# Turning the result by a VectorE block transpose and storing 64 short lines, in place of a PE product, a copy and 16 longer lines

## The chip, the cores and the metric

The kernel runs on one core of one Trainium2 chip. The metric is the device time of one execution in microseconds (us), median of several. Since the change concerns the last 2.5 us of 420, I also use a second measure, read from each trace: **the tail**, from the start of the VectorE instruction that reads the last product (tile `mT`) to the last semaphore count of the store.

Names: PE is the matrix engine, PSUM the memory that its products go to, SBUF the on-chip memory with 128 partitions; DVE is VectorE, ACT ScalarE, POOL GpSimd. SP is the engine that issues the loads and stores; an "issue" is its instruction for one of them. A "line" is one contiguous run of bytes of a transfer, and a "packet" is what the trace records of a DMA engine's work: here one line, or one count of the semaphore.

## The reference, cut to what matters

The program is one decode step for two sequences: a conditioning vector makes six modulation vectors, attention runs over a cache of 32768 keys and values, then an MLP. Only its last line matters here:

```python
x = x + ga * _A_ref(h, A_k_cache, A_v_cache, A_wq, A_wo)
h = _layernorm(x, axis=-1) * (1 + cb) + sb
x = x + gb * _B_ref(h, B_w1, B_b1, B_w2, B_b2)
return x            # bfloat16, (2, 1, 1024)
```

The result is 2 x 1024 bfloat16 numbers, 4 KB.

## The kernel before

The MLP's second product ends in PSUM with the features on partitions: feature 128k + p of sequence b stands at partition p, column (k, b). Memory wants a sequence's features one behind the other, so the result is turned, by a PE product with the identity, before it is stored.

```python
    for g in range(16, FT):                  # last product, waits for the last load
        ...
            pe(... e.matmul(psO[:, 2 * k:2 * k + 2], lhsT=w[:, j, k * 128:(k + 1) * 128], rhs=gT[:, g, 0:2], ...)
    dve(lambda e: e.tensor_tensor(mT[:, :, :], psO[:, 0:16].rearrange("p (k b) -> p k b", b=2), mod(5), ALU.mult), ...)
    dve(lambda e: e.tensor_tensor(res_bf.rearrange("p b k -> p k b"), mT[:, :, :], x1b[:, :, :], ALU.add), ...)
    pe(lambda e: e.matmul(psM[0:16, 0:128], lhsT=res_bf.rearrange("p b k -> p (b k)"), rhs=ident[:, :], start=True, stop=True), ...)
    dve(lambda e: e.tensor_copy(res16[:, :], psM[0:16, 0:128]), ...)

    s_out = nc.alloc_semaphore("s_out")
    T.wait("sp", reads=["res16"])
    T.raw("sp", lambda e: e.dma_start(out.rearrange("b o (k p) -> (b o k) p", p=128), res16[:, :]).then_inc(s_out, 16))
    ...
    nc.sync.wait_ge(s_out, 16)               # the program ends when the store has landed
```

`x1b` is the residual with the bias, ready some 13 us earlier.

## Time and profile before

| | before |
|---|---|
| time, three runs | 420.12 us (420.05 to 420.15) |
| span of the profiled run | 418.7 us |
| read from memory | 178.28 MB, 426 GB/s |
| last load's product, on PE | 413.27 to 416.18 us |
| two VectorE steps, PE turn, cast | 416.22 to 417.31 us |
| issue of the store to its landing | 1.35 us |

Read it from the bottom up: the kernel is a stream of loads, and after the last one there is a chain in which every instruction waits for the one ahead of it. The lines are shown in the prediction.

### The profile page before, as it was taken

What the parts mean: (1) busy time and instruction counts of PE and PEld (TensorE: products, weight loads), DVE (VectorE), ACT (ScalarE), POOL (GpSimd) and SP (SyncE); (2) the same over time, 40 slices, a digit from 0 to 9 for tenths busy, and PEclk for the clock granted to TensorE, in tenths of its full rate; (3) what the DMA queues carried; (4) which work ended last, traced back from release to release, by engine and by line L of the source; (5) the groups of instructions that cost most, each with busy time, mean ns of one, the idle gap of its engine ahead of it and who ended that gap; (6) DMA issues with size and microseconds to landing.
All of it is one profiled execution on the core that took longest, in us unless ns stands there. A gap on an engine that the chain in (4) does not pass through costs nothing.

```text
span 418.7 us, 11609 instructions
## 1 busy us (share of the span) xinstructions
PE 291.0 (70%) x5183; PEld 231.3 (55%) x5183; DVE 209.6 (50%) x423; ACT 149.4 (36%) x179; POOL 6.8 (2%) x29
## 2 busy tenths in 40 slices
PE   1407449766996895699369957976995699564536
PEld 1104219762993794299149926962894399221214
DVE  1201105546677676467726664766477567620411
ACT  2000015533565364256405632643365166400100
POOL 3000000000000000000000000000000000000000
PEclk9999557986896997799589958986697889576585
DMA  9989999999999999999999999999999999899995
GB/s 373 450 380 449 448 404 493 398 406 446 441 432 429 423 451 429 419 454 457 391 435 476 407 416 448 438 438 426 438 438 426 416 460 457 377 448 428 424 427 249
DMA packets 5581, 178.42 MB, mean 426 GB/s; under 512 B 698, under 2 KB 706, under 8 KB 964
## 3 DMA queue, kind: packets, MB, share of 16 engines
q1 hardware_dynamic: 5572, 178.28, 98.8%
q8 instruction: 8, 0.13, 0.1%
q14 instruction: 1, 0.01, 0.0%
HBM read 178.28 MB, written 0.00 MB: 426 GB/s over the span
## 4 chain that ended last, share of the span: by engine, by line
DMA 71%; PE 24%; DVE 2%; issue 1%; ACT 1%; SPq 1%
DMA V<-in_A_v_cache_dram 39%; DMA wo<-in_A_wo_dram 10%; DMA K<-in_A_k_cache_dram 10%; PE psZ L584 10%; DMA w<-in_B_w_dram 9%; PE psKT L536 8%; DMA wmod<-in_w_mod_dram 4%; PE psS L548 1%; PE psZ L548 1%; PE psS L655 1%; PE psZ L729 1%; PE psZ L469 1%; ACT KT_sb L540 0%; PE psS L469 0%; DVE m1c L553 0%
## 5 line engine op out<-in xcount | busy, mean ns | idle before, releaser
L536 PE MATMUL psKT<-ident,K 128*128 128x128 bf16 x2048 | 163.1, 229 | 11.5 <-DMA K<-in_A_k_cache_dram 11.5
L540 ACT ACTIVATE KT_sb<-psKT 128x1024 bf16<-128x1024 bf16 x96 | 98.2, 1025 | 124.4 <-PE psKT L536 124.4
L542 DVE COPY KT_sb<-psKT 128x1024 bf16<-128x1024 bf16 x160 | 106.7, 688 | 61.6 <-PE psKT L536 61.2
L536 PEld LDWEIGHTS psKT<-ident,K 128*128 128x128 bf16 x2048 | 126.7, 102 | 13.0 <-DMA K<-in_A_k_cache_dram 12.7
L584 PE MATMUL psZ<-V,E_sb 128*32 128x512 bf16 x512 | 46.4, 541 | 23.2 <-DMA V<-in_A_v_cache_dram 20.0
L548 PE MATMUL psS<-qcur,KT_sb 128*128 128x8 bf16 x1024 | 44.7, 167 | 2.2 <-issue 2.2
L584 PEld LDWEIGHTS psZ<-V,E_sb 128*32 128x32 bf16 x512 | 18.7, 130 | 47.7 <-issue 38.8
L548 PE MATMUL psZ<-qcur,KT_sb 128*128 128x8 bf16 x1024 | 43.0, 167 | 2.2 <-issue 1.5
L548 PEld LDWEIGHTS psS<-qcur,KT_sb 128*128 128x128 bf16 x1024 | 40.0, 97 | 2.3 <-issue 2.3
L548 PEld LDWEIGHTS psZ<-qcur,KT_sb 128*128 128x128 bf16 x1024 | 37.9, 96 | 3.4 <-issue 1.6
L572 ACT ACTIVATE E_sb<-S_sb 128x512 bf16<-128x512 f32 x32 | 19.5, 630 | 29.6 <-DVE S_sb L570 29.6
L570 DVE TENSOR_TENSOR S_sb<-S_sb,gmb 128x512 f32<-128x512 f32 x32 | 20.0, 685 | 0.3
L576 DVE TENSOR_REDUCE rs<-E_sb 128x8 f32<-128x512 bf16 x32 | 19.7, 675 | 0.0
L469 PE MATMUL psS<-wmod,inT 128*32 128x512 bf16 x32 | 5.1, 624 | 16.2 <-DMA wmod<-in_w_mod_dram 16.2
L553 DVE TENSOR_REDUCE m1c<-psZ 128x8 f32<-128x512 f32 x16 | 11.1, 693 | 10.2 <-ACT S_sb L552 10.1
L595 DVE RECIPROCAL rinv<-psM 128x1 f32<-128x1 f32 x8 | 1.3, 168 | 27.7 <-PE psM L593 27.7
L605 PE MATMUL psM<-msum,hmat 128*128 128x128 f32 x16 | 4.2, 347 | 13.3 <-DVE msum L600 13.3
L559 PE MATMUL psM<-identf,m 128*8 128x128 f32 x16 | 4.3, 369 | 13.1 <-DVE m L556 13.1
L553 DVE TENSOR_REDUCE m1c<-psS 128x8 f32<-128x512 f32 x16 | 11.1, 693 | 3.2 <-ACT S_sb L552 3.1
L552 ACT ACTIVATE S_sb<-psZ 128x512 f32<-128x512 f32 x16 | 9.5, 595 | 7.5 <-PE psZ L548 7.5
L477 DVE COPY S_sb<-psS 128x512 f32<-128x512 f32 x1 | 0.7, 690 | 22.9 <-PE psS L469 22.9
L469 PEld LDWEIGHTS psS<-wmod,inT 128*32 128x32 bf16 x32 | 1.1, 132 | 19.3 <-DMA wmod<-in_w_mod_dram 18.0
(123 smaller groups left out, 167.5 us busy)
## 6 DMA issues: line engine op xcount, KB each, us to landing
K<-in_A_k_cache_dram SPq DMA_DIRECT2D x16, 4096.0 KB, 27.1
wq<-in_A_wq_dram SPq DMA_DIRECT2D x2, 4096.0 KB, 44.8
wo<-in_A_wo_dram SPq DMA_DIRECT2D x2, 4096.0 KB, 39.0
w<-in_B_w_dram SPq DMA_DIRECT2D x2, 3584.0 KB, 32.5
wmod<-in_w_mod_dram SPq DMA_DIRECT2D x1, 6144.0 KB, 29.8
w<-in_B_w_dram SPq DMA_DIRECT2D x3, 2048.0 KB, 37.8
wmod<-in_w_mod_dram SPq DMA_DIRECT2D x1, 4608.0 KB, 15.8
wmod<-in_w_mod_dram SPq DMA_DIRECT2D x1, 1536.0 KB, 6.0
```

The costliest lines, as they stand in the source:

```text
L469: pe(lambda e, w=it.view, k=k, kk=kk, ch=ch, n=n, q=q: e.matmul(bank[n][32 * q:32 * q + 32, :], lhsT=inT[:, k, :], rhs=w[:, kk, ch * 512:( ...
L536: pe(lambda e, kq=kq, jj=jj, w=kt, t=t: e.transpose(psKT[kq][:, jj * 128:(jj + 1) * 128], w[:, t, :], ident[:, :]), reads=[it.reg, "ident" ...
L540: act(lambda e, src=src: e.activation(KT_sb[g8][:, :, :], src, ACT.Copy), reads=[f"psKT{kq}"], writes=[f"KT_sb{g8}"], sem=f"ev{cc}_{g8}")
L542: dve(lambda e, src=src: e.tensor_copy(KT_sb[g8][:, :, :], src), reads=[f"psKT{kq}"], writes=[f"KT_sb{g8}"], sem=f"ev{cc}_{g8}")
L548: pe(lambda e, t=t, jj=jj: e.matmul(ps[:, t * HPG:(t + 1) * HPG], lhsT=KT_sb[g8][:, jj, :], rhs=qcur[:, :], start=True, stop=True), reads= ...
L552: act(lambda e: e.activation(Sc, ps.rearrange("p (t h) -> p h t", h=HPG), ACT.Copy), reads=[preg], writes=[f"S_sb_{cc}"], sem=f"sc{cc}")
L553: dve(lambda e: e.tensor_reduce(m1c[:, :, cc], ps.rearrange("p (t h) -> p h t", h=HPG), AX.X, ALU.max), reads=[preg], writes=[f"m1c{cc}"])
L559: pe(lambda e: e.matmul(psM[0:HPG, 0:128], lhsT=m1[:, :], rhs=identf[:, :], start=True, stop=True), reads=["m1", "identf"], writes=["psM"])
L570: dve(lambda e: e.tensor_tensor(Sc, Sc, gmb[:, :].unsqueeze(2).to_broadcast([128, HPG, TPC]), ALU.subtract), reads=[f"S_sb_{cc}", "gmb"], ...
L572: act(lambda e: e.activation(Ec, Sc.rearrange("p h (u t) -> p u h t", t=4), ACT.Exp, scale=SCALE), reads=[f"S_sb_{cc}"], writes=[f"E_sb_{c ...
L576: dve(lambda e: e.tensor_reduce(rs4[:, :, cc], Ec.rearrange("p u h t -> p h u t"), AX.XY, ALU.add), reads=[f"E_sb_{cc}"], writes=[f"rs4_{c ...
L584: pe(lambda e, t4=t4, tg=tg, q=q: e.matmul(psO[32 * q:32 * q + 32, :], lhsT=E_sb[:, tg // 4, :, :].rearrange("p h t -> p (h t)"), rhs=vt[: ...
```

## The change

The intent is to take the detour over PE and PSUM out of that chain. One VectorE instruction transposes 32x32 blocks within the partitions, so four blocks of 32 partitions are turned at once; the 16 columns are spread to 32, every second one zero, so that one even step selects the 64 lines. Each line has 32 numbers, 64 bytes, and the store puts them at their places.

```diff
-    res_bf = sb("res_bf", [128, 2, KT8], BF16)
-    res16 = c16
+    res_bf = sb("res_bf", [128, 2, KT8, 2], BF16)
+    resT = sb("resT", [128, 32], BF16)
@@ (at the start)
+    T.inst("pool", lambda e: e.memset(res_bf[:, :, :, :], 0.0), writes=["res_bf"])
@@ (at the end; the semaphore wait is on resT then)
-    dve(... tensor_tensor(res_bf.rearrange("p b k -> p k b"), mT, x1b, ALU.add) ...)
-    pe(... matmul(psM[0:16, 0:128], lhsT=res_bf.rearrange("p b k -> p (b k)"), rhs=ident[:, :], ...) ...)
-    dve(... tensor_copy(res16[:, :], psM[0:16, 0:128]) ...)
+    dve(... tensor_tensor(res_bf[:, :, :, 0].rearrange("p b k -> p k b"), mT, x1b, ALU.add) ...)
+    dve(... transpose(resT[:, :], res_bf.rearrange("p b k e -> p (b k e)")) ...)
-    T.raw("sp", ... dma_start(out.rearrange("b o (k p) -> (b o k) p", p=128), res16[:, :]) ...)
+    T.raw("sp", ... dma_start(out.rearrange("b o (k q r) -> q (b o k) r", q=4, r=32), resT[0:128:2, :]) ...)
```

More of the change, by code (lines that the diff above doesn't have):

```diff
@@ L732, in bass_adaLN_cond__gqa_block_cached__mixer_channel_mlp__decode_kernel @@
     dve(lambda e: e.tensor_tensor(mT[:, :, :], psO[:, 0:16].rearrange("p (k b) -> p k b", b=2), mod(5), ALU.mult), reads=["psO", "modT"], writes=["mT"])
-    dve(lambda e: e.tensor_tensor(res_bf.rearrange("p b k -> p k b"), mT[:, :, :], x1b[:, :, :], ALU.add), reads=["mT", "x1b"], writes=["res_bf"])
-    pe(lambda e: e.matmul(psM[0:16, 0:128], lhsT=res_bf.rearrange("p b k -> p (b k)"), rhs=ident[:, :], start=True, stop=True),
-       reads=["res_bf", "ident"], writes=["psM"])
-    dve(lambda e: e.tensor_copy(res16[:, :], psM[0:16, 0:128]), reads=["psM"], writes=["res16", "c16"])
+    dve(lambda e: e.tensor_tensor(res_bf[:, :, :, 0].rearrange("p b k -> p k b"), mT[:, :, :], x1b[:, :, :], ALU.add), reads=["mT", "x1b"], writes=["res_bf"])
+    dve(lambda e: e.transpose(resT[:, :], res_bf.rearrange("p b k e -> p (b k e)")), reads=["res_bf"], writes=["resT"])
     s_out = nc.alloc_semaphore("s_out")
-    T.wait("sp", reads=["res16"])
-    T.raw("sp", lambda e: e.dma_start(out.rearrange("b o (k p) -> (b o k) p", p=128), res16[:, :]).then_inc(s_out, 16))
+    T.wait("sp", reads=["resT"])
+    T.raw("sp", lambda e: e.dma_start(out.rearrange("b o (k q r) -> q (b o k) r", q=4, r=32), resT[0:128:2, :]).then_inc(s_out, 16))
     with nc.Block(no_gpsimd_drain=True) as block:
```

## The prediction

> **What bounds the kernel now.** I read the page first, then the chain of waits in its last stretch, then the timeline of the last 2.5 us, then the DMA view of the last 1.4 us. The page's summary of the chain that ended last says what the whole kernel is made of, and its DMA rows say how the store behaves:
>
> ```profile
> span 418.7 us, 11609 instructions
> ...
> DMA 71%; PE 24%; DVE 2%; issue 1%; ACT 1%; SPq 1%
> ```
>
> The kernel reads 178.28 MB at 426 GB/s and is a stream of loads with some PE work that isn't hidden. Nothing of the change touches that stream. So the question is what happens after the last load has landed. The timeline of the end shows it (start, duration, then engine, line and tile):
>
> ```profile
> 413.27 2.91 PE L729 MATMUL psZ<-gT,w 128*128 128x2 bf16 x96 [0.30 <-DMA w<-in_B_w_dram]
> 416.22 0.17 DVE L732 TENSOR_TENSOR mT<-psZ,modT 128x16 f32<-128x16 f32 x1 [5.17 <-PE psZ L729]
> 416.43 0.23 DVE L733 TENSOR_TENSOR res_bf<-mT,x1b 128x16 bf16<-128x16 f32 x1
> 416.72 0.09 PEld L734 LDWEIGHTS psM<-ident,res_bf 128*16 128x16 bf16 x1 [0.62 <-DVE res_bf L733]
> 416.72 0.28 PE L734 MATMUL psM<-ident,res_bf 128*16 128x128 bf16 x1 [0.53 <-DVE res_bf L733]
> 417.03 0.28 DVE L736 CAST c<-psM 16x128 bf16<-16x128 f32 x1 [0.37 <-PE psM L734]
> 417.34 0.35 SPq L740 DMA_DIRECT2D out_dram<-c  x1
> ```
>
> Here the reader is to see that every instruction waits for the one above it: nothing overlaps from 416.22 us on. The chain of waits in the same stretch lists the same five steps with the small gaps between the engines, which is why I count the gaps too:
>
> ```profile
> 416.43 0.24 DVE res_bf L733
> 416.68 0.04 issue
> 416.72 0.29 PE psM L734
> 417.01 0.02 issue
> 417.03 0.28 DVE c L736
> ```
>
> After that comes the store, and it is a third of this tail. It is issued at 417.34 us and its row of DMA issues gives 1.4 us to landing, which ends at 418.7 us, the end of the span. The waits of the queue's own engine end on it too:
>
> ```profile
> out_dram<-c SPq DMA_DIRECT2D x1, 4.0 KB, 1.4
> ...
> SPq L744 <- DMA out_dram<-c: 0.6, 1, 0.6
> ```
>
> The second line is the last wait of the program: SP waits for the store's semaphore. All engines have met at the end of the block 0.6 us earlier, so freeing PE or VectorE earlier there gains nothing by itself; only an earlier landing does. The DMA view of 417.3 to 418.7 us, 40 slices of 35 ns, shows where the 1.4 us go:
>
> ```profile
> DMA  0000000000000000000000000111100000000000
> GB/s 0 0 0 0 0 0 0 0 0 0 0 0 0 0 0 0 0 0 0 0 0 0 0 0 0 37 15 37 22 8 0 0 0 0 0 0 0 0 0 0
> DMA packets 32, 0.00 MB, mean 3 GB/s; under 512 B 32, under 2 KB 32, under 8 KB 32
> ```
>
> Some 0.85 us pass before the first packet, 32 packets (16 of 256 bytes and 16 small ones that count the semaphore) lie within five slices, some 0.17 us, and another 0.35 us pass until the last count has arrived. In the packet records a 256-byte packet took 15 ns and a counting one 9 ns, so the 0.17 us are mostly the start of one engine after the other.
>
> **What the Trainium skill says.** (1) "VectorE: DVE Perf Modes", section "The three transpose paths": a VectorE transpose of 128x128 bf16 takes 311 ns against 390 ns by TensorE, it transposes 32x32 blocks only and writes to SBUF. The trace before has one such transpose, in f32 out of PSUM (L704, 128x896, 1.12 us), which agrees in kind: 896 elements at about 1.04 ns are 0.93 us, which leaves some 0.19 us of fixed cost. (2) "DMA: Bandwidth & Descriptors", section "Why a DMA increments its semaphore by 16 and not by 1": a DMA is spread over the largest k up to 16 engines that divides the slowest dimension of both access patterns. The trace agrees for the store of before: 16 lines on either side, 16 data packets and 16 counts. [...](4) The same page, "Specifications": below 512 bytes a transfer is a read-modify-write. No record here shows it; the lines of before, 256 bytes, are already below, so the change doesn't cross that limit.
>
> **The change part by part.** *Removed:* the gap of 0.04 us to PE, the product (0.29 us in the chain), the gap of 0.02 us back and the cast (0.28 us): 0.63 us, from 416.68 to 417.31 us. The semaphore hop to SP (417.31 to 417.34 us) stays.
>
> *Added on the path:* one VectorE transpose, 128x32 bf16. From L704 I take 0.19 us fixed plus 32 x 1.04 ns = 0.03 us, so 0.22 us. The skill's 311 ns for 128 columns, less 96 x 1.04 ns, gives 0.21 us. The gap between two dependent VectorE instructions is 0.03 us (L732 ends at 416.40, L733 starts at 416.43). So 0.25 us stand where 0.63 us stood: **0.38 us less**.
>
> *Altered on the path:* L733 writes every second element now. It took 231 ns, while L421 with the same sizes and a bf16 output of adjacent pairs took 175 ns. The old output has stepped single 2-byte writes; the new one has too, but no two share 4 bytes. I count 0 and allow up to 0.06 us less.
>
> *The store:* the result in memory is addressed as 4 x 16 x 32 elements, whose slowest dimension is 4; the SBUF side has 64 lines. By the skill's rule k falls from 16 to 4, so each of four engines gets 16 packets of 64 bytes and one count, in a row. A 64-byte packet is between 9 ns (4 bytes) and 15 ns (256 bytes), say 10 to 12 ns: 17 x 11 = 0.19 us per engine, plus about 0.04 us until the fourth has started (0.145 us for 16 engines before, 0.01 us each), so 0.23 us where 0.17 us stood: 0.06 us more. Had k stayed 16, it would be about 0.2 us, hardly different. To this I add another 0.07 us, a guess, for writing out four times as many descriptors and for the receipts of 16 writes per engine instead of one. In all the store costs **about 0.13 us more**, with room for 0.4.
>
> *Hidden:* a POOL memset of 128x32 bf16 at the start. The inT memset of 128x256 took 0.31 us and ended at 2.45 us, and its first reader on VectorE runs at 7.98 us, held by a load; 0.1 us more on POOL isn't seen. SBUF addresses behind the buffer move by some tens of bytes; I count 0.
>
> *Sum:* -0.38 + 0.13 = -0.25 us. The time before is 420.12 us (three runs within 0.10 us), so **419.87 us**.
>
> **The rivals.** *First: the store gives it all back.* 64 short lines on four engines take 0.4 us longer than 16 lines on sixteen, by slower descriptor making or by slow partial writes to memory. For it: the time to landing is most of the tail, and its 0.85 us before the first packet are a stage of which the trace shows nothing inside. Against it: loads of 128 lines were issued in 0.33 us, hardly different from the 0.35 us of this 16-line store, and packets are small against the fixed parts. It would make 420.1 to 420.5 us. *Second: the store costs nothing more*, since the short packets overlap with the receipts and the start of sixteen engines falls away; with the faster L733 the gain is 0.4 to 0.45 us, so 419.7 us. *Third: another wait takes the place of the removed one*: the meeting of the engines at the end of the block. It ends 0.6 us before the landing now, and starts earlier with the store, so it can't become the last. *Fourth: the stream moves by itself*, through shifted buffers or the TensorE clock (0.50 granted in the last stretch, 0.81 in the mean). A shift of one part in a thousand is 0.4 us, more than the whole effect; three runs of before within 0.1 us speak against it within one kernel, but not between two builds.
>
> **Range and chances.** The removed part is known to 0.05 us, the store's addition lies between 0 and 0.4 us, and the stream can add about 0.3 us either way. That gives 419.4 to 420.4 us for 8 in 10. Two per cent are 8.4 us, while the whole tail after the last product is 2.5 us, so faster by over 2% is out of reach by this change, and slower by as much needs an accident outside it: 0.99 for the same.
>
> **What would show it.** Right: after L733 a VectorE transpose of 0.20 to 0.24 us, 0.03 us behind it; no PE instruction after L729; the store's issue 0.35 to 0.45 us sooner after the end of L729; 68 packets in the last 1.5 us if k is 4 (80 if it is 16), within 0.2 to 0.3 us; 1.5 us to landing. Wrong: a time to landing of 1.8 us or more (first rival), or a start of L732 that differs from 416.22 us by more than 0.3 us (fourth).

## The result, and the profile after

The changed kernel takes 420.21 us (420.15 to 420.38, six runs), the kernel before in the same rounds 420.13 us (420.04 to 420.23). The ratio is 1.0003, with a 95% interval of 0.9990 to 1.0016: the same, and the 0.08 us between the medians is not clear of the noise.

The timeline of the end, changed kernel (start, duration, engine, line, operation and tile):

```profile
416.19 0.17 DVE L733 TENSOR_TENSOR mT<-psZ,modT 128x16 f32<-128x16 f32 x1 [5.18 <-PE psZ L730]
416.40 0.23 DVE L734 TENSOR_TENSOR res_bf<-mT,x1b 128x16 bf16<-128x16 f32 x1
416.66 0.21 DVE L735 STREAM_TRANSPOSE resT<-res_bf 128x32 bf16<-128x32 bf16 x1
416.90 0.65 SPq L739 DMA_DIRECT2D out_dram<-resT  x1
```

PE is gone from the chain and the transpose is as short as hoped: the store is issued at 416.90 instead of 417.34 us. Counted from the start of `mT`, that is 0.711 us instead of 1.115, so **0.404 us are gained**. But the issuing instruction itself is busy for 0.65 us instead of 0.35. The DMA view of 416.9 to 418.3 us, which starts with the issue and has 40 slices of 35 ns like the one of before:

```profile
DMA  0000000000000000000000000000000000000233
GB/s 0 0 0 0 0 0 0 0 0 0 0 0 0 0 0 0 0 0 0 0 0 0 0 0 0 0 0 0 0 0 0 0 0 0 0 0 9 26 35 33
```

The first packets lie in slice 36, some 1.28 us after the issue, where the kernel before had 0.85 us. The wider view counts 68 packets, 64 of data and 4 that count the semaphore: four engines share the store. The last packet starts 0.171 us after the first (0.157 before), and the last count arrives 0.394 us after that (0.347 before). Together the landing comes 1.843 us after the issue instead of 1.352: **0.491 us are given back**, of which 0.430 lie ahead of the first packet. The tail is 2.554 us instead of 2.467.

### The profile page after: what moved, and what is told of

Read it like the earlier page. It is cut to its first block, busy times and chain, and to the rows that moved or that the text cites. A ratio compares the mean times of both kernels' runs of the same rounds, so it can differ in the third digit from the quotient of the medians.

```text
span 418.8 us, 11608 instructions
## 1 busy us (share of the span) xinstructions
PE 288.9 (69%) x5182; PEld 231.1 (55%) x5182; DVE 209.6 (50%) x423; ACT 149.1 (36%) x179; POOL 6.8 (2%) x30
## 4 chain that ended last, share of the span: by engine, by line
DMA 79%; PE 18%; issue 1%; DVE 1%; SPq 1%; ACT 1%
DMA V<-in_A_v_cache_dram 47%; DMA K<-in_A_k_cache_dram 10%; DMA wo<-in_A_wo_dram 10%; PE psZ L585 9%; DMA w<-in_B_w_dram 9%; PE psKT L537 4%; DMA wmod<-in_w_mod_dram 4%; PE psS L549 1%; PE psZ L730 1%; PE psZ L549 1%; PE psZ L470 1%; PE psS L656 0%; PE psS L470 0%; SPq L648 0%; ACT KT_sb L541 0%
## 5 line engine op out<-in xcount | busy, mean ns | idle before, releaser
L537 PE MATMUL psKT<-ident,K 128*128 128x128 bf16 x2048 | 161.3, 227 | 13.0 <-DMA K<-in_A_k_cache_dram 13.0
L537 PEld LDWEIGHTS psKT<-ident,K 128*128 128x128 bf16 x2048 | 125.0, 101 | 14.4 <-DMA K<-in_A_k_cache_dram 14.4
L585 PE MATMUL psZ<-V,E_sb 128*32 128x512 bf16 x512 | 45.2, 530 | 25.9 <-DMA V<-in_A_v_cache_dram 24.2
```

Of the source, the lines that this page charges most:

```text
L537: pe(lambda e, kq=kq, jj=jj, w=kt, t=t: e.transpose(psKT[kq][:, jj * 128:(jj + 1) * 128], w[:, t, :], ident[:, :]), reads=[it.reg, "ident" ...
L585: pe(lambda e, t4=t4, tg=tg, q=q: e.matmul(psO[32 * q:32 * q + 32, :], lhsT=E_sb[:, tg // 4, :, :].rearrange("p h t -> p (h t)"), rhs=vt[: ...
```

## The experiments

All traces with one store at the end, side by side (e8 has four and is told below). "Plain" is one step from line to line in memory, "nested" are two. Times in us, from the trace's instruction, packet and semaphore records; "first", "last" and "landing" are the first packet, the start of the last packet and the last semaphore count, counted from the start of the issue. "Engines" is the number of counting packets.

| run | lines x bytes | partitions | pattern in memory | engines | issue took | first | last | landing | tail |
|---|---|---|---|---|---|---|---|---|---|
| before | 16 x 256 | neighbours | plain | 16 | 0.346 | 0.848 | 1.005 | 1.352 | 2.467 |
| after | 64 x 64 | every second | nested 4 x 16 | 4 | 0.649 | 1.278 | 1.449 | 1.843 | 2.554 |
| e1 | 64 x 64 | every second | plain | 16 | 0.549 | 1.192 | 1.367 | 1.719 | 2.435 |
| e2 | 62 x 64 | every second | plain | 2 | 0.702 | 1.328 | 1.566 | 2.026 | 2.741 |
| e3 | 64 x 64 | every second | nested 16 x 4 | 16 | 0.644 | 1.289 | 1.459 | 1.815 | 2.528 |
| e4 | 16 x 256 | neighbours | nested 4 x 4 | 4 | 0.740 | 1.374 | 1.491 | 1.832 | 2.894 |
| e5 | 64 x 64 | neighbours | plain | 16 | 0.530 | 1.176 | 1.346 | 1.697 | 2.411 |
| e6 | 16 x 64 | every second | plain | 16 | 0.590 | 1.232 | 1.381 | 1.718 | 2.432 |
| e7, second use | 64 x 64 | every second | nested 4 x 16 | 4 | 0.537 | 1.169 | 1.340 | 1.731 | 2.507 |
| e9 | 16 x 256 | neighbours | plain | 16 | 0.346 | 0.842 | 0.998 | 1.346 | 2.061 |
| e10 | 16 x 128 | neighbours | plain | 16 | 0.346 | 0.838 | 0.994 | 1.325 | 2.039 |
| e11 | 16 x 64 | neighbours | plain | 16 | 0.347 | 0.844 | 0.995 | 1.319 | 2.031 |
| e12 | 16 x 256 | neighbours | plain | 16 | 0.327 | 0.830 | 0.985 | 1.339 | 2.187 |

The table also shows two classes. From the end of the issuing instruction to the first packet ("first" less "issue took") it is 0.49 to 0.50 us in the five rows of 16 plain lines from neighbouring partitions, and 0.63 to 0.65 us in all others. So of the extra time ahead of the first packet, some 0.14 us come after the issue and are alike in every slow form; the rest is in the issue itself and differs from form to form.

The first theories were A, the nested pattern makes the issue long; B, the number of lines; C, the few engines.

**e1: a plain pattern in memory.**

```diff
-  out.rearrange("b o (k q r) -> q (b o k) r", q=4, r=32), resT[0:128:2, :]
+  out.rearrange("b o (n r) -> (b o n) r", r=32), resT[0:128:2, :]
```

> The changed kernel with its 64 lines of 64 bytes laid one behind the other in memory (a wrong order of the result, on purpose): same lines, same SBUF side, but one plain step between lines instead of two nested ones. Theory A (the nested 4 x 16 pattern makes the issue long): issue back at about 0.35 us, first packet 0.85 us after it, landing about 1.4 us after it, and since the issue stays 0.44 us sooner than before, the time is about 0.4 us under the kernel before, 419.75 us. Theory B (64 lines instead of 16): stays at 0.65 us of issue, 1.28 us to the first packet, 1.84 us to the landing, 420.2 us. Theory C (four engines instead of sixteen): as A, since 64 lines on both sides allow 16 engines.

The issue took 0.549 us, the first packet came at 1.192. Between the theories: with a plain pattern and 16 engines the store is only 0.10 us of issue shorter, and far from 0.346. Neither A nor C alone explains the loss. B had said that nothing would change, so it misses 0.10 us too. The time was 420.13 us against 420.06 (ratio 1.0002, interval 0.9988 to 1.0015); the 0.03 us by which the tail is under that of before can't be seen in it.

**e2: 62 plain lines, which only two engines can share.**

```diff
+  out.rearrange("b o (n r) -> (b o n) r", r=32)[0:62, :], resT[0:124:2, :]
```

> As the flat store, but 62 lines, which only 2 engines can share (the last 64 numbers stay unwritten, on purpose). Theory A (nested pattern): issue 0.35 us, first packet 0.85 us after it; the packets then take 31 x 7 ns = 0.22 us per engine. Theory C (few engines): issue 0.65 us or more, first packet 1.28 us or later. Theory B (lines): as C.

0.702 us of issue and 1.328 to the first packet: 0.15 and 0.14 us over e1, whose only other difference is two lines more. So the few engines cost something here, as far as one trace of each shows. The landing is 0.31 us later than in e1: 0.14 us ahead of the first packet, 0.06 us from the first to the last packet (31 lines for each engine), and 0.11 us behind it.

**e3: nested, but shared by 16 engines.**

```diff
+  out.rearrange("b o (n r) -> (b o n) r", r=32).rearrange("(j i) r -> i j r", j=4), resT[0:128:2, :]
```

> 64 lines of 64 bytes in a nested pattern whose slow dimension is 16 (16 x 4 instead of 4 x 16; wrong order on purpose), so that 16 engines share it. Theory A (nested pattern): issue 0.65 us, first packet about 1.28 us after it, 80 packets. Theory C (four engines): issue 0.35 us, first packet 0.85 us after it. Theory B (lines): as A.

0.644 and 1.289 us with 80 packets: like the changed kernel, within 0.01 us, though 16 engines work. So in the nested pattern, four engines in place of sixteen cost nothing ahead of the first packet and 0.03 us at the landing. C is not what costs here; the nesting is worth 0.10 us over e1.

**e4: the kernel before, only its 16 lines permuted, so that the store is nested 4 x 4 (a right result).**

```diff
-  res_bf.rearrange("p b k -> p k b") ...
+  res_bf.rearrange("p b k -> p (b k)").rearrange("p (j b i) -> p i j b", b=2, i=2) ...      # inputs likewise
-  out.rearrange("b o (k p) -> (b o k) p", p=128), res16[:, :]
+  out.rearrange("b o (i j p) -> j (b o i) p", j=4, p=128), res16[:, :]
```

> The kernel before with its PE product and cast, 16 lines of 256 bytes, but the lines permuted so that the store has a nested pattern of 4 x 4 lines (a right result): only the store's pattern changes. Theory A (nested pattern): issue 0.65 us instead of 0.35, first packet 0.4 us later, time 0.4 us over the kernel before, 420.55 us. Theory B (64 lines): nothing changes, 420.13 us. Theory C (four engines): slower as in A, or by the part that the engines make.

The last line of its timeline:

```profile
417.40 0.74 SPq L740 DMA_DIRECT2D out_dram<-c  x1
```

With PE and cast untouched and 16 lines of 256 bytes, the issue takes 0.74 us in place of the 0.35 of before. The landing is 0.48 us later, and the time 420.76 us (420.71 to 420.89) against 420.06, ratio 1.0018 (1.0004 to 1.0031). This run shows in the time itself that the form of a 4 KB store costs something, without VectorE's transpose and without short lines; how much is read from the trace: the landing's 0.48 us, less 0.05 us for a shorter VectorE sum, make the tail 0.43 us longer. The rest of the 0.70 us isn't in the tail. The run doesn't part A from C: with the pattern, the engines fell from 16 to four as well (20 packets), and 16 lines nested over 16 engines were not tried.

B had now failed in e4 and A in e1, so no single one of the two would do, and the step between partitions came in as theory D, the first use of a form as theory W.

**e5: 64 lines from neighbouring partitions.**

```diff
+  out.rearrange("b o (n r) -> (b o n) r", r=32), resT[0:64, :]
```

> As the flat store of 64 lines of 64 bytes, but read from 64 neighbouring partitions instead of every second one (wrong numbers, on purpose). The flat store of e1 took 0.55 us of issue and 1.19 us to the first packet with 64 lines and stepped partitions. Theory B (number of lines): stays at 0.55 and 1.19 us. Theory D (every second partition): falls to about 0.35 and 0.85 us. Theory W (a form of transfer that the program hasn't used before is slow the first time): as D, since plain neighbouring lines are what all loads use.

```profile
417.04 0.53 SPq L739 DMA_DIRECT2D out_dram<-resT  x1
```

0.530 and 1.176 us, only 0.02 less than e1. With 64 lines the step between partitions makes hardly a difference.

**e6: 16 lines from every second partition.**

```diff
+  out.rearrange("b o (n r) -> (b o n) r", r=32)[0:16, :], resT[0:32:2, :]
```

> 16 lines of 64 bytes from every second one of 32 partitions, plain in memory (the rest of the result stays unwritten, on purpose). Theory B (number of lines): 0.35 us of issue, 0.85 us to the first packet. Theory D (every second partition): 0.55 and 1.19 us.

```profile
416.96 0.59 SPq L739 DMA_DIRECT2D out_dram<-resT  x1
```

0.590 and 1.232 us. 16 lines alone don't help either, and this form is a little slower than 64 lines. B can't be the whole cause. Taken with e5, each looks like a refutation of the other theory; what was missing was the run with neither step nor 64 lines (e11).

**e7: the same store once before.**

```diff
+    T.raw("sp", ... dma_start(out.rearrange("b o (k q r) -> q (b o k) r", q=4, r=32), resW[0:128:2, :]).then_inc(s_warm, 16))
+    T.raw("sp", lambda e: e.wait_ge(s_warm, 16))
     T.wait("sp", reads=["resT"])
```

> The changed kernel, and some 40 us before the end, while SP is idle, the same store once from a zeroed buffer, with its own semaphore and waited for (a right result). Theory W (first use is slow): the last store is issued in about 0.4 us, its first packet comes about 0.9 us after, landing about 1.45 us after, the time is 419.8 us. Theories A, B and D (the form itself is slow each time): 0.65, 1.28 and 1.84 us as without it, 420.2 us.

```profile
L742 SPq DMA_DIRECT2D out_dram<-resW x1: 650/650/650, 375.6 to 375.6; - x1
L745 SPq DMA_DIRECT2D out_dram<-resT x1: 537/537/537, 417.2 to 417.2; - x1
```

The first use took 0.650 us, the last 0.537, and its landing came 1.731 us after the issue instead of 1.843. So W has a share of 0.11 us in this run, and most of the extra stays. The store was also issued 0.07 us later after `mT` than in the changed kernel, which the experiment may have brought in itself. The time, 420.21 us against 420.05 (1.0004, 0.9990 to 1.0017), shows no gain.

**e8: four plain stores, two from SP and two from ACT (a right result).**

```diff
+    for q in range(4):
+        T.raw("sp" if q < 2 else "act", lambda e, q=q: e.dma_start(dst4[q], resT[32 * q:32 * q + 32:2, :]).then_inc(s_out if q < 2 else s_out2, 16))
```

> The changed kernel with the store cut into four of 16 lines, one for each block of 32 partitions, two from SP and two from ACT (a right result). If a plain 16-line store costs 0.35 us of issue and 1.35 us to landing (B), the second of each queue lands about 1.7 us after the first issue, 0.14 us sooner than the one nested store: 0.1 us under both kernels in the tail. If stepped partitions are slow (D), the second is issued 0.55 us later and lands about 2.2 us after: 0.35 us slower than the changed kernel.

The tile view of the store (durations in ns, smallest, median and largest):

```profile
L743 SPq DMA_DIRECT2D out_dram<-resT x2: 576/583/590, 417.0 to 417.6; - x2
L743 ACTq DMA_DIRECT2D out_dram<-resT x2: 594/722/849, 417.0 to 417.6; - x2
```

Each issue costs 0.58 us or more again, the second of a queue as well, so first use isn't what makes this form slow here. ACT's second took 0.85 us and landed last: the tail is 3.340 us, the time 421.20 us against 420.05, ratio 1.0028 (1.0015 to 1.0042). A worse version, as D had it, and worse than D's number.

**e9, e10, e11: 16 neighbouring partitions, lines of 256, 128 and 64 bytes, behind the VectorE transpose.**

```diff
-    resT = sb("resT", [128, 32], BF16)
+    resT = sb("resT", [128, 128], BF16)      # e10: 64 columns, e11: 32; zeroed at the start where wider
+    ... out.rearrange("b o (k p) -> (b o k) p", p=128), resT[0:16, :]
+    ... out.rearrange("b o (k p) -> (b o k) p", p=64)[0:16, :], resT[0:16, :]      # e10
+    ... out.rearrange("b o (k p) -> (b o k) p", p=32)[0:16, :], resT[0:16, :]      # e11
```

> The changed kernel with its transpose, but what is stored is 16 lines of 256 bytes from 16 neighbouring partitions of a widened buffer (wrong numbers, on purpose): VectorE's part of the change alone, with the store of the kernel before. So far every store of 64-byte lines took 0.53 to 0.70 us of issue, also with 16 lines, also from neighbouring partitions, also on 16 engines. Theory S (the 64-byte line makes it long): issue 0.35 us, first packet 0.85 us, landing 1.35 us after the issue, which stays 0.4 us sooner than before: the tail from the start of the last product's reader to the landing is 2.06 us, the time 419.7 us. Theory P (what the store reads or when it is issued makes it long, not its form): 0.55, 1.19 and 1.7 us as the other stores after a transpose.

> As the run with 256-byte lines, but 16 lines of 128 bytes (half of the result stays unwritten, on purpose). Theory S with a gradual size effect: between 0.35 and 0.59 us of issue; with a limit between 64 and 128 bytes: 0.35 us; with a limit between 128 and 256: 0.59 us. Theory P: 0.55 us or more.

> As the run with 256-byte lines, but 16 lines of 64 bytes, from 16 neighbouring partitions. Theory S: as the run with stepped partitions, 0.59 us of issue, 1.23 us to the first packet. If the step and not the size made that one slow: 0.35 and 0.85 us. Theory P: 0.55 us or more.

The issue of e9, then that of e11 with its DMA view of 416.92 to 418.32 us, again from the issue on:

```profile
416.98 0.35 SPq L740 DMA_DIRECT2D out_dram<-resT  x1
```

```profile
416.92 0.35 SPq L739 DMA_DIRECT2D out_dram<-resT  x1
...
DMA  0000000000000000000000001010000000000000
GB/s 0 0 0 0 0 0 0 0 0 0 0 0 0 0 0 0 0 0 0 0 0 0 0 0 14 6 6 6 0 0 0 0 0 0 0 0 0 0 0 0
```

All three are issued in 0.35 us, with the first packet in slice 24, after 0.84 us. The length of a line, theory S, does nothing, and where the data come from, theory P, does nothing. **e11 and e6 differ in one thing, 16 partitions side by side against every second of 32**, and that is 0.35 against 0.59 us of issue and 0.401 us in the tail. e11 and e5 differ in 16 against 64 lines: 0.35 against 0.53 us. So the step alone and the number alone each cost some 0.2 us of issue, and both together no more than that (e1: 0.55).

e9 also shows VectorE's part of the change in the time: 419.65 us (419.48 to 419.72) against 420.06, ratio 0.9990 (0.9976 to 1.0003). That interval just reaches 1, but every run of it was under every run of before (419.96 to 420.19), and the 0.41 us of the medians are the 0.406 us of the tails.

**e12: a version meant to beat both, and the forms once more.** No form of the change's store that I found is plain on 16 neighbouring partitions and right, so this goes the other way: keep the store of before and take another step out of the chain. The residual is put into PSUM early by a PE product, and the last product adds to it.

```diff
+    pe(... matmul(psM[0:16, 0:128], lhsT=x1b.rearrange("p b k -> p (b k)"), rhs=identf[:, :], start=True, stop=False, ...))   # early
-    dve(... tensor_tensor(mT, psO, mod(5), ALU.mult)); dve(... tensor_tensor(res_bf, mT, x1b, ALU.add))
+    dve(... tensor_tensor(res_bf[:, :, :], psO[:, 0:16].rearrange("p (k b) -> p b k", b=2), mod(5).rearrange("p k b -> p b k"), ALU.mult))
-    pe(... matmul(psM[0:16, 0:128], lhsT=res_bf..., rhs=ident[:, :], start=True, stop=True))
+    pe(... matmul(psM[0:16, 0:128], lhsT=res_bf..., rhs=ident[:, :], start=False, stop=True, ...))
@@ and 14 stores of 64-byte lines to a scratch tensor, issued by SP behind the last loads
```

> Two things in one kernel. First, a version that should beat both (a right result): the kernel before with its PE product and its store of 16 lines of 256 bytes, but the residual x1b is put into the same PSUM bank by a PE product some 13 us before the end, so that the last product adds to it and the separate VectorE sum (0.23 us and a 0.03 us gap) leaves the path. Expected: 2.20 us from the start of the last product's reader to the landing, against 2.47 before and 2.55 with the change; time 419.85 us. Second, while SP is idle behind the last loads, 14 small stores to a scratch tensor, seven forms with 64-byte lines, each twice, which nothing waits for before the last store: 16 lines from neighbouring partitions, 16 from every second, 32, 64 and 128 from neighbouring ones, the nested 4 x 16 of the change, and a nested 4 x 4 of 16 lines. Only their issue times count, since they queue behind loads. Theory D (a step between partitions is what is slow): 0.35 us for all neighbouring plain ones, more for the second form. Theory L (a line count that was not used before, or 64 itself): 64 lines slow, 16 and 128 fast. Theory W (first use of a form): in each form the second issue is at 0.35 to 0.45 us, whatever the first was. If the form itself costs, first and second agree within 0.1 us, nested forms at 0.55 us or more both times.

Its timeline at the end:

```profile
416.22 0.17 DVE L736 TENSOR_TENSOR res_bf<-psZ,modT 128x16 bf16<-128x16 f32 x1 [5.23 <-PE psZ L733]
...
416.45 0.28 PE L737 MATMUL psM<-ident,res_bf 128*16 128x128 bf16 x1 [0.27 <-DVE res_bf L736]
416.76 0.28 DVE L739 CAST c<-psM 16x128 bf16<-16x128 f32 x1 [0.37 <-PE psM L737]
417.06 0.33 SPq L758 DMA_DIRECT2D out_dram<-c  x1
```

One VectorE instruction less, the store as before: the tail, counted from `res_bf` here, which now reads the last product, is 2.187 us against 2.467. The time is 419.77 us (419.63 to 419.85) against 419.99 (419.87 to 420.09), with a right result. All five runs are under all nine of before, yet the interval of the ratio, 0.9995 (0.9981 to 1.0008), doesn't exclude 1; the tail is the stronger evidence. The scratch stores are in this kernel too, so the version without them was not timed.

The second half of this run failed as a measurement. The tile view of the 14 scratch stores says why:

```profile
L755 SPq DMA_DIRECT2D scratch<-resW x14: 431/990/9895, 377.0 to 411.8; - x14
```

From the fourth on, an issue took up to 9.9 us: SP was held up behind the loads, so the durations are no longer those of the forms. Only the first three, issued at the pace of the loads around them (0.43 us each), may be read, and with care: 16 neighbouring lines 0.431 us (0.347 in e11), 16 with a step 0.594 (0.590 in e6), 32 neighbouring 0.649. The first is as long as the loads just ahead of it, which is 0.08 us over e11. The third hints that 32 lines are slow as well, but stands right before the hold-up.

## Why the prediction was right or wrong

The predicted time was 419.87 us with a range of 419.4 to 420.4; measured were 420.21 us, in the range, and "the same". That is no proof of the mechanism: the range was 1.0 us wide and held "no gain" too. The forecast gain of 0.25 us did not come: +0.08 us in the time, which noise could make, and +0.087 us in the tail. One term is to blame.

- **The VectorE part was right.** Predicted: 0.38 us less. Measured: 0.404 us in the trace, and 0.41 in the time where the store is left alone (e9). The transpose took 211 ns (predicted 220 from L704; the prediction's 0.21 us from the skill's 311 ns is an estimate that fits as well), the gaps are as small as said.
- **L733, now L734, was left at 0 and that was right:** 229 ns after 231.
- **The store was the mis-sized term.** In the words of the prediction it would cost "about 0.13 us more"; it cost 0.491. The 0.06 us for packets on four engines was even too much: from the first to the last packet it is 0.014 us more. The receipts are 0.047 us more. What failed is the guess of 0.07 us for "writing out four times as many descriptors" and for the receipts: 0.477 us were measured for the two, 0.430 of them ahead of the first packet. The reason that the prediction gave against it, that loads of 128 lines are issued in 0.33 us, compared numbers of lines and not forms of the pattern; those loads also go the other way, with lines of 2 KB and more, and took 0.33 us only where SP had waited for a free buffer first (0.35 to 0.52 us elsewhere).
- **So the first rival came true**, at 0.49 us instead of 0.4, and so did the prediction's own sign of being wrong, "a time to landing of 1.8 us or more" (1.843). The place fits its arm of slower descriptor making, ahead of the packets; that it is the making of descriptors is not shown. Its other arm, slow partial writes, did not: lines of 256, 128 and 64 bytes land alike (e9, e10, e11: 1.346, 1.325 and 1.319 us).
- **The engine count was right** (68 packets, four engines), and of little weight: 0.03 us at the landing (e3).
- **No other wait took over** and the POOL memset wasn't seen, as said. The stream moved by some 0.2 us between traces, as allowed for.

What stays open: why the forms cost what they cost. Step, number of lines and nesting don't add up (a step alone +0.24 us of issue, 64 lines alone +0.18, both +0.20, both and nesting +0.30, nesting with four engines on 16 lines +0.39, which e4 doesn't part), and the large loads of 128 lines, at 0.33 us, fit no rule by number of lines that would hold for loads too. No store of more than 16 long lines was run. That the preparation of the store, ahead of its packets, is where the time goes is shown; what inside it is slow is not.

## What to carry to other kernels

When the last thing a kernel does is a small store, its fixed time is part of the critical path, and the form of its access pattern is part of that fixed time: count from the issue to the first packet, not the packets. Of the forms tried here, one line on each of 16 neighbouring partitions, laid out plainly in memory, was 0.32 to 0.54 us quicker to its first packet than any other, so look for steps to remove from the chain that keep that form. Where an effect is a thousandth of the time, measure the stage in the trace and change one property of it at a time.

## What the Trainium skill lacked or had wrong

- "DMA: Bandwidth & Descriptors", "Anatomy of one DMA", describes the path issued from GpSimd and calls descriptor making small, with many descriptors possible before its cost shows. It doesn't carry over to the stores issued from SP here: 64 lines instead of 16 moved the first packet from 0.844 to 1.176 us after the issue, a step between the partitions to 1.232 (e11, e5, e6). No run here issues from GpSimd, so the passage itself isn't tested. I found no figure on the page for SP's path by the form of the pattern.
- The same page's rule for the number of engines (section "Why a DMA increments its semaphore by 16 and not by 1") was right for the last store of every trace, down to the odd case of 62 lines on two engines (64 packets). The section says that the issuing engine writes the counts of the unused engines itself, at once; the traces agree, with one more count 0.41 us after the end of the issue and ahead of the first packet wherever fewer than 16 engines work (after, e2, e4, e7). What the page lacks is whether few engines lengthen the issue on this chip: 0.702 against 0.549 us (e2, e1), though not in the nested form (0.649 against 0.644), and the loads of `b2m`, 1 to 4 lines on 1 to 4 engines by their counts, were issued in 0.25 to 0.29 us.
- "SBUF — State Buffer", in the section "Door 1", says that an access that moves to another 16-byte line pays a penalty. It gives no size for a small VectorE instruction: the bf16 sum that writes alternately to addresses 16 or 32 bytes apart took 231 and 229 ns, and the same sum with writes 4 bytes apart took 179 ns (e4), which agrees. With f32 writes 32 bytes apart the penalty is far smaller, 178 against 168 ns (`x1b` in e12 and before), so these runs give no rule for it.
